# A routing step's scatter list moved ahead of filler products, and two one-element writes into the expert buffers' pool

## The chip, the core and the metric

The kernel runs on one core of one Trainium2 chip. The metric is the device time of one execution in microseconds (us); before and after are run several times on the same chip. The core's engines are TensorE (PE, with its weight loads shown apart as PEld), VectorE (DVE), ScalarE (ACT), GpSimd (POOL) and SyncE (SP), and 16 DMA engines move data between device memory and the core's memory. Each engine works through its own instructions in the order in which the program gives them.

## The reference

Linear attention with an exponential feature map feeds a mixture of eight experts. The part that this change touches is the second half:

```python
logits = x @ w_gate                      # x: 4608 tokens x 512
for idx in np.argsort(-logits.flatten()):
    tok, e = idx // E, idx % E
    if assigned[tok] >= 0 or counts[e] >= cap: continue   # cap = 4608 // 8 = 576
    assigned[tok] = e; counts[e] += 1
for e in range(E):
    mask = assigned == e
    h = np.maximum(x[mask] @ w1[e], 0.0)     # 512 -> 1024
    out[mask] = h @ w2[e]                    # 1024 -> 512
```

Every token goes to one expert and every expert takes exactly 576 tokens. The greedy rule is followed exactly, in eight rounds: a round finds the expert that fills up next, the threshold at which it does, and the list of its 576 tokens.

## The kernel before, in words

**Stages.** The attention part comes first and writes its result `xs` (4608 x 512) to device memory. Then `routing(0)` finds the first expert and its tokens. While expert `r` is computed, `routing(r+1)` runs between its instructions, mostly on VectorE. The first routing (`wide`) has nothing to run beside: nothing else can start until it has named an expert.

**What `routing(0)` does.** Six digits of the threshold are found one after the other (the loop over `i`): VectorE compares (L602), TensorE counts (L614), VectorE tests the counts (L631) and picks (L639, L643). Then the tokens are ranked and a list of 576 row numbers is made: compares against the low digit in `lo` (L701), 18 products with `hv` (L709) whose sum is copied to `pb` (L714), and eight small products (L719) that spread `pb` over the partitions. Two casts write the list into `idx[:,0:4]` and `idx[0:64,4]` (L720, L721). The list has five blocks: four of 128 tokens and a remainder of 64. The remainder's results are scattered as half rows, so the scatter needs a list of its own, `idx[:,5]`: four more products with one column (L742) and one VectorE instruction (L743). Only the scatter of the remainder reads it. Behind it stand the steps that take the expert's tokens out of the game (L744 to L752); they change `L`, from which `routing(1)` starts (L435).

**Fillers.** `idle(n)` (L581) issues n products on constant ones into a bank that nobody reads. Eleven of them stand between the eight list products (L719) and the four of the remainder (L742); four and three stand behind the first two transposes.

**The expert part.** `ga` (L852) gathers a block of rows from `xs` into `xg` with an indirect DMA that GpSimd issues; five gathers make an expert. Behind the second gather of expert 0 GpSimd copies the expert's number (L818), and on that copy SP waits before it issues the last two of the four parts of `w1` (`raww`, L766). ScalarE casts each part to its high half (`w1h`, L837) and VectorE forms the low half (`w1l`, L840, two instructions a part). For blocks 0 and 1 TensorE transposes `xg` (L882), ScalarE casts (`xh`, L895 and L894), VectorE subtracts (`xl`, L897); blocks 2 and 3 are transposed together (L887). The products of the first layer (L922) are three times split: `xh*w1h`, `xh*w1l`, `xl*w1h`. ScalarE applies the relu (`fh`, L935) and VectorE forms the low half (`fl`, L939), which also frees the PSUM bank. The second layer is L953, and the results are scattered by indirect DMAs (L983).

**Order.** The order of the expert part is written out by hand: a table gives every step a place, and each engine follows its own sequence. On ScalarE the casts of the third and fourth part of `w1` come ahead of the first relu. On VectorE the steps of `routing(1)` alternate with `w1l`, `xl` and `fl`. `up0`, which holds L742 to L752, is VectorE's first step.

**Pools.** The tiles of the expert part lie in the pool `fp`, which takes over memory of the attention part's tiles. The first instruction of an engine that writes a tile of `fp` therefore has to wait for the last users of that memory: other engines and many DMA queues. The small tiles of the routing lie in another pool (`rt`), which was there from the start. The tile `wk` is one of those: a GpSimd copy of one element (L705) that waits for the first group of `lo`.

Of the kernel before, what the change touches and what calls it, by code (L numbers as in the profile page):

```python
# [9 lines left out]
BF = mybir.dt.bfloat16  # L10
I32 = mybir.dt.int32
AF = mybir.ActivationFunctionType
OP = mybir.AluOpType
# [545 lines left out]
def moe(ctx, tc, nc, L, xs, w1, w2, out, C, MC, R0, rt, cfg={}):  # L559
# [3 lines left out]
    V,G,A,PE=nc.vector,nc.gpsimd,nc.scalar,nc.tensor  # L563
    rp=rt
    fp=ctx.enter_context(tc.tile_pool(name='ffn',bufs=2))
# [3 lines left out]
    def inner(x,n): return x.rearrange('p (t o) -> p t o',o=1).to_broadcast([x.shape[0],x.shape[1],n])  # L569
    def mid(x,t): return x[:,None,:].to_broadcast([x.shape[0],t,x.shape[1]])  # L570
# [3 lines left out]
    S=lambda shape,name,dt=F32,b=1: rp.tile(shape,dt,name=name,bufs=b)  # L574
    def rps(shape): return ps.tile(shape,F32,name='rps',bufs=cfg.get('rps',2))
# [6 lines left out]
    def routing(r):  # L582

        last = r==E-1
        wide = r<cfg.get('wide',1)
        if not last:
            R=R0 if r==0 else state()
            if r: yield from prep(R,0,NT)
            dg,OH=R['dg'],R['OH']
            c=dg[:,0]; lat=cfg.get('lat0',1.2)  # L590
            for i,(sh,bits) in enumerate(DIG):
                K=KW[i]; n=128//K; fin=i==ND-1
                part='n0' in R and i==0
                if part:
                    p=rps([8,K])
                    cnt0(R,p,NT//9-1,cmp0(R,NT//9-1),True,True)
                else:
                    cmp=S([128,NT//n,K,n],f'cmp{K}',BF,b=2)
                    cv=c.rearrange('p (g i) -> p g i',i=n)
                    g=0  # L600
                    for ck in ((WC if K==32 else WC2) if wide else (9,)*(1 if K==32 else 2)):
                        V.tensor_tensor(cmp[:,g:g+ck],cv[:,g:g+ck,None,:].to_broadcast([128,ck,K,n]),  # L602
                                        kt[i].rearrange('p (k i) -> p k i',i=n)[:,None].to_broadcast([128,ck,K,n]),op=OP.is_ge); g+=ck
                if 'rest' in R:
                    with tc.issue_after(R['last']):
                        if i: 
                            for _ in R.pop('rest'): pass
                        else: next(R['rest'])
                yield
                if part: pass  # L610
                elif wide:
                    p=rps([8,K])
                    for t in range(NT):
                        PE.matmul(p,OH[:,t,:],cmp[:,t//n,:,t%n],start=t==0,stop=t==NT-1)  # L614
                else:
                    p=rps([128,n,8])
                    for g in range(NT//n):
                        PE.matmul(p,cmp[:,g].rearrange('p k i -> p (k i)'),OH[:,g*n:g*n+n,:],start=g==0,stop=g==NT//n-1)  # L618
                    yield
                    mm=S([128,n,8],f'mm{n}'); V.tensor_mul(mm,p,msk[n])  # L620
                    V.tensor_reduce(tin[:,0:8].rearrange('p (e o) -> p e o',o=1),mm.rearrange('p i e -> p e i'),axis=AX.X,op=OP.add)
                    tr=S([128,32],'tr'); V.transpose(tr,tin)
                    yield
                    cn8=S([128,32//n,1],f'cn{n}'); V.tensor_reduce(cn8,tr.rearrange('p (k i) -> p k i',i=n),axis=AX.X,op=OP.add)
                    f32=S([128,32//n],f'f{n}'); V.tensor_scalar(f32,cn8[:,:,0],float(cap),2.0**(-7*i),op0=OP.is_ge,op1=OP.mult)
                    ds8=S([128,1],'ds'); V.tensor_reduce(ds8,f32,axis=AX.X,op=OP.add)
                if wide:
                    fl=S([8,K],f'fl{K}',BF); da=S([8,1],'da',BF)
                    with nc.allow_low_precision(reason='counts up to 64'):
                        if part: V.scalar_tensor_tensor(fl,p,-float(cap),R['n0'],op0=OP.add,op1=OP.is_ge,accum_out=da)  # L630
                        else: V.tensor_scalar(fl,p,float(cap),0.0,op0=OP.is_ge,op1=OP.add,accum_out=da)  # L631
                else:
                    fl=S([128,8],'fl128',BF); V.tensor_scalar(fl,eye8,ds8,None,op0=OP.mult)
                yield
                p=rps([128,8])
                if wide: PE.matmul(p,da.to_broadcast([8,128]),e8s[:,i],start=True,stop=True)
                else: PE.matmul(p,ones,fl,start=True,stop=True)
                if r: yield
                ch=S([128,1],'ch'); V.tensor_reduce(ch,p,axis=AX.X,op=OP.max)  # L639
                lat=cfg.get('latd',.7)  # L640
                if fin: break
                c2=S([128,NT],'cc',BF,b=2)
                V.scalar_tensor_tensor(c2,c,ch,dg[:,i+1],op0=OP.subtract,op1=OP.add); c=c2  # L643
                if r: yield

            f8=S([128,8],'f8')
            V.scalar_tensor_tensor(f8,p,ch,e8,op0=OP.is_equal,op1=OP.mult)
            c1=S([128,1],'c1'); V.tensor_scalar(c1,ch,-2.0**(-7*(ND-1)),None,op0=OP.add)
            mx=S([128,1],'mx'); V.tensor_reduce(mx,f8,axis=AX.X,op=OP.max)
        else:  # L650
            f8=S([128,8],'f8'); V.tensor_mul(f8,opn,e8)
            mx=S([128,1],'mx'); V.tensor_reduce(mx,f8,axis=AX.X,op=OP.max)
# [19 lines left out]
        p=rps([128,2,NT])  # L672
# [23 lines left out]
        if r: yield  # L696
        lo=S([128,18,64,2],'cmp64',BF,b=2)
        l2=sf[:,0].rearrange('p (g i) -> p g i',i=2)
        lk=6 if wide else 9
        for g in range(0,18,lk):  # L700
            V.tensor_tensor(lo[:,g:g+lk],l2[:,g:g+lk,None,:].to_broadcast([128,lk,64,2]),  # L701
                            kl.rearrange('p (k i) -> p k i',i=2)[:,None].to_broadcast([128,lk,64,2]),op=OP.is_equal)
        if wide:

            wk=S([1,1],'wk',BF); G.tensor_copy(wk,lo[0:1,0,0,0:1])  # L705
        yield
        p=rps([128,9,2,2])
        for g in range(18):
# [2 lines left out]
        idx=S([128,6,1],'idx',I32,b=3)  # L711
        if wide:

            pb=S([128,9,2,2],'pb',BF); V.tensor_copy(pb,p)  # L714
            p=rps([128,5])
            for j in range(4):
                for o in (0,64):
                    k=5 if o==0 else 4
                    PE.matmul(p[o:o+64,0:k],dup2[:,j%2,o:o+64],pb[:,o//64:9:2,j//2,j%2],start=j==0,stop=j==3,skip_group_check=True)  # L719
            V.tensor_copy(idx[:,0:4,0],p[:,0:4])  # L720
            V.tensor_copy(idx[0:64,4,0:1],p[0:64,4:5])  # L721
        else:

            pm=S([128,9,2,2],'pm')
            V.tensor_mul(pm,p,msk[2][:,:,0][:,None,None,:].to_broadcast([128,9,2,2]))
            d9=S([128,9,2,1],'d9',BF)
            with nc.allow_low_precision(reason='under 64, and multiples of 64 up to 71 times 64'): V.tensor_reduce(d9,pm,axis=AX.X,op=OP.add)
            yield
            p=rps([128,9,2])
            PE.matmul(p,dup.rearrange('p i a -> p (i a)'),d9[:,:,:,0],start=True,stop=True)  # L730
            yield
            pr=S([128,9,2],'pr'); V.tensor_copy(pr,p)
            V.tensor_add(idx[0:64,0:5,0],pr[0:64,0:9:2,0],pr[0:64,0:9:2,1])
            V.tensor_add(idx[64:128,0:4,0],pr[64:128,1:9:2,0],pr[64:128,1:9:2,1])
            r8=S([128,1],'r8'); V.tensor_add(r8,pr[:,8,0:1],pr[:,8,1:2])
            V.tensor_scalar(idx[:,5],r8,2.0,half,op0=OP.mult,op1=OP.add)
        T['idx',r]=idx
        if not last:
            yield 'up'
            if wide:  # L740
                p=rps([128,1])
                for j in range(4): PE.matmul(p,dup2[:,j%2],pb[:,8:9,j//2,j%2],start=j==0,stop=j==3)  # L742
                V.tensor_scalar(idx[:,5],p,2.0,half,op0=OP.mult,op1=OP.add)  # L743
            E1=S([128,8],'E1'); V.tensor_scalar(E1,f8,mx,None,op0=OP.is_equal)  # L744
            mem=S([128,NT],'mem'); g1=S([128,NT],'g1')
            V.tensor_add(g1,gt[:,0],gt[:,1])
            V.scalar_tensor_tensor(mem,si,12288+cap-.5,g1,op0=OP.is_lt,op1=OP.mult)
            V.tensor_sub(un,un,mem)
            V.tensor_sub(opn,opn,E1)
            pen=S([128,NT,8],'sc')  # L750
            V.tensor_tensor(pen,inner(mem,8),mid(E1,NT),op=OP.max)
            V.scalar_tensor_tensor(L,pen,-1.0e38,L,op0=OP.mult,op1=OP.add)  # L752
    BL=[(b*128,min(128,cap-b*128)) for b in range(5)]
    ctx.enter_context(tc.manual_schedule())

    it0=routing(0)
    for x in it0:
        if x=='ei':
# [296 lines left out]
```

## Time and profile before

| | |
|---|---|
| time, median of 3 runs | 763.65 us (763.33 to 764.94) |
| time of the profiled execution | 765.09 us |
| its span, first to last instruction | 763.2 us |
| TensorE products busy | 736.1 us (96%) |
| TensorE weight loads busy | 633.3 us (83%) |
| VectorE busy | 571.4 us (75%) |
| ScalarE busy | 348.2 us (46%) |
| GpSimd busy | 312.0 us (41%) |
| mean granted TensorE clock | 0.977 |

The profiled execution is read in microseconds from its first instruction. Attention ends near 277 us, the first routing near 301 us, and the first expert's products begin at 307 us. A busy share is an average over stages with different limits; what the change touches lies between 277 and 330 us.

### The profile page before, as it was taken

How to read it: one execution, taken by the hardware profiler on the slowest of the kernel's cores; microseconds unless marked ns; L12 is line 12 of the kernel's file. 1: busy time of each engine (PE TensorE's matmuls, PEld its weight loads, DVE VectorE, ACT ScalarE, POOL GpSimd, SP SyncE). 2: the span in 40 equal slices, each digit the busy share in tenths (PEclk: the TensorE clock that was granted, in tenths of full speed). 3: DMA queues.
4: the chain of work that ended last, by engine and by line, in shares of the span. 5: the costliest groups of instructions: out<-in, count | busy, mean ns of one | idle time of the engine just before them, and what ended most of it. 6: DMA issues, size and time to landing. Idle time of an engine off the chain costs nothing.

```text
span 763.2 us, 25319 instructions
## 1 busy us (share of the span) xinstructions
PE 736.1 (96%) x10832; PEld 633.3 (83%) x10832; DVE 571.4 (75%) x1495; ACT 348.2 (46%) x612; POOL 312.0 (41%) x336
## 2 busy tenths in 40 slices
PE   7999999999999966999999999999999999999997
PEld 3888888998898864788897897897897897897985
DVE  5999899989997975996796796796796795673410
ACT  2677677877788431333522422422422422542411
POOL 6797888988889701103103103103103103312002
PEclk9999999999999985999999999999999999999999
DMA  9979688988883032325405405406405406662301
GB/s 168 153 136 154 132 166 165 165 142 156 156 167 81 13 86 75 104 107 186 160 1 182 164 2 183 163 1 186 160 1 184 163 2 198 236 190 60 132 15 49
DMA packets 236944, 94.28 MB, mean 124 GB/s; under 512 B 185904, under 2 KB 223184, under 8 KB 236832
## 3 DMA queue, kind: packets, MB, share of 16 engines
q1 hardware_dynamic: 225552, 71.91, 40.4%
q0 software_dynamic: 6608, 20.16, 8.3%
q8 instruction: 85, 1.39, 0.8%
q10 hardware_dynamic: 4672, 0.59, 0.6%
q14 instruction: 27, 0.22, 0.1%
HBM read 72.58 MB, written 20.05 MB: 121 GB/s over the span
## 4 chain that ended last, share of the span: by engine, by line
PE 65%; issue 13%; DVE 12%; POOL 4%; ACT 2%; SPq 2%; DMA 1%; POOLq 0%; DVEq 0%
PE h L922 22%; PE y L953 18%; PE g L293 8%; DVE kgm L189 4%; PE y L968 3%; PE g L185 3%; PE g L276 2%; PE g L231 2%; SPq L122 2%; DVE qgt L192 2%; DVE qgm L189 2%; PE rps L618 2%; POOL ks L222 1%; PE g L247 1%; PE h L887 1%
## 5 line engine op out<-in xcount | busy, mean ns | idle before, releaser
L983 POOL DMA_INDIRECT out_dram<-ysb,idx x40 | 39.2, 981 | 335.9 <-ACT ysb L976 329.9
L222 POOL TENSOR_TENSOR ks<-ks,kP 128x512 f32<-128x512 f32 x112 | 143.2, 1279 | 7.4 <-ACT kP L213 0.2
L922 PE MATMUL h<-xh,w1l 128*128 128x272 f32 (+3 forms) x512 | 142.0, 297 | 0.3 <-DVE w1l L840 0.2
L922 PE MATMUL h<-xh,w1h 128*128 128x272 f32 (+3 forms) x512 | 141.6, 302 | 0.1
L935 ACT ACTIVATE fh<-h 128x272 fp32r<-128x272 f32 (+2 forms) x128 | 49.1, 384 | 136.6 <-PE h L922 128.8
L953 PE MATMUL y<-w2h,fh 128*128 128x512 f32 x256 | 101.2, 398 | 0.0
L953 PE MATMUL y<-w2l,fh 128*128 128x512 f32 x256 | 99.9, 395 | 0.0
L953 PE MATMUL y<-w2h,fl 128*128 128x512 f32 x256 | 99.3, 392 | 0.0
L922 PEld LDWEIGHTS h<-xh,w1l 128*128 128x128 f32 x512 | 97.1, 190 | 1.8 <-DVE w1l L840 0.8
L922 PEld LDWEIGHTS h<-xh,w1h 128*128 128x128 f32 x512 | 96.0, 190 | 2.0 <-issue 0.4
L922 PE MATMUL h<-xl,w1h 128*128 128x272 f32 (+3 forms) x512 | 93.3, 299 | 1.1 <-DVE xl L897 1.1
L213 ACT ACTIVATE kP<-kgt 128x768 f32<-128x768 f32 x96 | 73.9, 837 | 34.0 <-POOL kgt L201 19.0
L939 DVE SCALAR_TENSOR_TENSOR fl<-h,fh 128x272 fp32r<-128x272 f32 (+2 forms) x128 | 53.0, 416 | 38.7 <-ACT fh L935 22.2
L293 PE MATMUL g<-kz,qP 128*64 128x73 f32 x2304 | 78.9, 229 | 2.0 <-DVE kz L262 1.8
L293 PEld LDWEIGHTS g<-kz,qP 128*64 128x64 f32 x2304 | 76.3, 138 | 3.8 <-DVE kz L262 1.9
L280 ACT ACTIVATE qP<-g 128x768 f32<-128x768 f32 x96 | 70.9, 813 | 16.1 <-PE g L276 16.1
L922 PEld LDWEIGHTS h<-xl,w1h 128*128 128x128 f32 x512 | 76.5, 190 | 1.8 <-DVE xl L897 1.3
L231 PE MATMUL g<-kP,vi 64*64 64x256 f32 x1152 | 70.5, 377 | 0.1
L976 ACT COPY ysb<-y 128x512 f32<-128x512 f32 (+1 forms) x40 | 21.8, 546 | 100.5 <-issue 59.2
L953 PEld LDWEIGHTS y<-w2l,fh 128*128 128x128 f32 x256 | 48.2, 188 | 9.0
L953 PEld LDWEIGHTS y<-w2h,fl 128*128 128x128 f32 x256 | 48.2, 188 | 8.8
L953 PEld LDWEIGHTS y<-w2h,fh 128*128 128x128 f32 x256 | 48.3, 189 | 8.3
(220 smaller groups left out, 1314.7 us busy)
## 6 DMA issues: line engine op xcount, KB each, us to landing
raww<-in_moe_w_dram SPq DMA_DIRECT2D x64, 512.0 KB, 5.2
xs<-xp SPq DMA_DIRECT2D x32, 288.0 KB, 4.7
ki<-in_k_dram SPq DMA_DIRECT2D x62, 144.0 KB, 3.9
qi<-in_q_dram SPq DMA_DIRECT2D x62, 144.0 KB, 4.0
vi<-in_v_dram SPq DMA_DIRECT2D x56, 144.0 KB, 4.1
vi<-in_v_dram POOLq DMA_DIRECT2D x8, 144.0 KB, 7.2
xl<-xd SPq DMA_DIRECT2D x4, 288.0 KB, 4.3
xd<-xg SPq DMA_DIRECT2D x4, 256.0 KB, 3.5
```

What stands on the lines that cost most here:

```text
L185: PE.matmul(p[64*bi:64*bi+64,a,128*(s-s0):128*(s-s0)+128],t[r,bi,s,:],C['w'][r,:],start=True,stop=True)
L189: V.tensor_reduce(m,vw(),axis=AX.X,op=OP.max,apply_absolute_value=True)
L213: for i in range(2): A.activation(o[:,:,:,128*i:128*i+128],t,AF.Exp,scale=1.0-2*i)
L222: else: G.tensor_add(ks,ks,kP[:,s])
L231: PE.matmul(p[64*a:64*a+64,i,0:256],v_[r,a,s,:],kP[r,s,a,:],start=s==0,stop=s==8,skip_group_check=True)
L280: for fh in range(2): A.activation(t[:,fh].rearrange('p i a s t -> p i (a s t)'),p,AF.Exp,scale=1.0-2*fh)
L293: PE.matmul(p[64*ab:64*ab+64,a,73*(j-j0):73*(j-j0)+73],T['qP',u,j//3][:,fh,a,ab,j%3,:],T['kz',u][:,a,fh,ab,:],start=fh==0,stop=fh==1)
L922: PE.matmul(p,ws[:,k,o:o+128],xx[:,k,o1:o2],start=n==0,stop=n==11)
L935: A.activation(hh[:,f,o1:o1+m1],p[:,0:m1],AF.Relu)
L939: V.scalar_tensor_tensor(hl[:,f,o1:o1+m1],p[:,0:m1],0.0,hh[:,f,o1:o1+m1],op0=OP.max,op1=OP.subtract)
L953: PE.matmul(p,hx[:,f,o:o+128],ws[:,f%2,:],start=n==0,stop=n==23)
L983: st=G.indirect_dma_start(out=ov,out_offset=bass.IndirectOffsetOnAxis(ap=iv,axis=0),in_=yv,in_offset=None)
```

## The change

Four edits. The four products and the VectorE instruction that make `idx[:,5]` move from behind the eleven fillers to the place behind the eight list products, under the same `routing(0)`. The tile `wk` moves from the routing's pool to `fp`. In the fourth of the six digit steps (`i==3`) VectorE writes a zero into a new one-element tile `wv` of `fp`. The 18 rows of `lo` are compared in groups of 7, 7 and 4 instead of three of 6.

```diff
@@ routing, the loop over the digits @@
                         V.tensor_tensor(cmp[:,g:g+ck],cv[:,g:g+ck,None,:].to_broadcast([128,ck,K,n]),
                                         kt[i].rearrange('p (k i) -> p k i',i=n)[:,None].to_broadcast([128,ck,K,n]),op=OP.is_ge); g+=ck
+                if wide and i==3: V.memset(fp.tile([1,1],BF,name='wv',bufs=1),0.0)
@@ routing, the list @@
-        lk=6 if wide else 9
-        for g in range(0,18,lk):
+        g0=0
+        for lk in (7,7,4) if wide else (9,9):
+            g=g0; g0+=lk
             V.tensor_tensor(lo[:,g:g+lk],l2[:,g:g+lk,None,:].to_broadcast([128,lk,64,2]),
                             kl.rearrange('p (k i) -> p k i',i=2)[:,None].to_broadcast([128,lk,64,2]),op=OP.is_equal)
         if wide:
-            wk=S([1,1],'wk',BF); G.tensor_copy(wk,lo[0:1,0,0,0:1])
+            wk=fp.tile([1,1],BF,name='wk',bufs=1); G.tensor_copy(wk,lo[0:1,0,0,0:1])
@@ behind the eight list products @@
+            p5=rps([128,1])
+            for j in range(4): PE.matmul(p5,dup2[:,j%2],pb[:,8:9,j//2,j%2],start=j==0,stop=j==3)
             V.tensor_copy(idx[:,0:4,0],p[:,0:4])
             V.tensor_copy(idx[0:64,4,0:1],p[0:64,4:5])
+            V.tensor_scalar(idx[:,5],p5,2.0,half,op0=OP.mult,op1=OP.add)
@@ behind the fillers @@
             yield 'up'
-            if wide:
-                p=rps([128,1])
-                for j in range(4): PE.matmul(p,dup2[:,j%2],pb[:,8:9,j//2,j%2],start=j==0,stop=j==3)
-                V.tensor_scalar(idx[:,5],p,2.0,half,op0=OP.mult,op1=OP.add)
```

## Rows read from the trace of the kernel before

**Rows 1.** Windows: us, PE, PEld, DVE, ACT, POOL busy; clock, DMA share, GB/s
```profile
311.00:314.50 3.50, 3.50 (x18) 3.50 (x19) 3.50 (x13) 1.41 (x3) 0.00 (x0) 0.52 0.20 69
...
320.00:330.00 10.00, 9.90 (x89) 9.51 (x88) 9.20 (x33) 3.66 (x10) 0.00 (x0) 1.00 0.58 211
...
352.00:400.00 48.00, 48.00 (x420) 42.55 (x418) 37.25 (x126) 19.21 (x43) 8.59 (x13) 1.00 0.31 110
```

**Rows 2.** Timeline, TensorE: start us, us, line, tile, count, idle before and releaser
```profile
300.28 4.51 PE L581 MATMUL y<-onesb 128*128 128x512 bf16 x11
304.63 0.24 PE L742 MATMUL rps<-pb,dup 128*128 128x1 bf16 x4
304.98 0.66 PE L882 MATMUL h<-ident,xg 128*128 128x128 f32 x4
...
307.37 0.41 PE L922 MATMUL h<-xh,w1h 128*128 128x256 f32 x1
...
310.88 1.04 PE L922 MATMUL h<-xl,w1h 128*128 128x256 f32 x4 [1.06 <-DVE xl L897]
...
316.95 0.71 PE L887 MATMUL h<-ident,xg 64*128 64x64 f32 x16
...
318.77 0.28 PE L922 MATMUL h<-xh,w1l 128*128 128x256 f32 x1
```

**Rows 3.** Timeline, VectorE, the first routing and the first expert
```profile
286.55 0.18 DVE L631 TENSOR_SCALAR_CACHE_REDUCE fl<-rps 8x32 bf16<-8x32 f32 x1 [0.73 <-PE rps L614]
...
300.38 0.16 DVE L720 CAST idx<-rps 128x4 int32<-128x4 f32 x1 [0.47 <-PE rps L719]
...
304.91 0.22 DVE L743 TENSOR_SCALAR idx<-rps,half 128x1 int32<-128x1 f32 x1 [4.30 <-PE rps L742]
...
307.13 0.69 DVE L840 TENSOR_TENSOR w1l<-raww,w1h 128x512 fp32r<-128x512 f32 x1 [0.31 <-issue]
...
310.15 0.68 DVE L897 TENSOR_TENSOR xl<-h,xh 128x512 fp32r<-128x512 f32 x1
...
313.83 0.75 DVE L602 TENSOR_TENSOR cmp<-dg,kt 128x1152 bf16<-128x1152 bf16 x1
314.74 0.76 DVE L939 SCALAR_TENSOR_TENSOR fl<-h,fh 128x256 fp32r<-128x256 f32 x2 [0.16 <-ACT fh L935]
...
316.26 0.19 DVE L620 TENSOR_TENSOR mm<-rps,msk 128x32 f32<-128x32 f32 x1 [0.17 <-PE rps L618]
...
317.92 0.69 DVE L840 TENSOR_TENSOR w1l<-raww,w1h 128x512 fp32r<-128x512 f32 x1
```

**Rows 4.** Timeline, GpSimd: gathers of experts 0 and 2, a scatter
```profile
301.47 1.06 POOL L852 DMA_INDIRECT xg<-xs,idx  x1 [2.63 <-DMA raww<-in_moe_w_dram]
...
305.44 0.95 POOL L852 DMA_INDIRECT xg<-xs,idx  x1 [0.30 <-issue]
...
346.85 1.02 POOL L983 DMA_INDIRECT out_dram<-ysb,idx  x1 [39.14 <-ACT ysb L976]
...
414.73 1.50 POOL L852 DMA_INDIRECT xg<-xs,idx  x1 [0.30 <-issue]
```

**Rows 5.** Timeline, ScalarE, the same stretch, and the copy ahead of that scatter
```profile
300.91 1.99 ACT L837 CAST w1h<-raww 128x1024 fp32r<-128x1024 f32 x2 [2.81 <-DMA raww<-in_moe_w_dram]
305.67 0.59 ACT L895 CAST xh<-h 128x512 fp32r<-128x512 f32 x1 [2.78 <-PE h L882]
307.05 0.77 ACT L894 CAST xh<-h 128x128 fp32r<-128x128 f32 x4 [0.79 <-PE h L882]
...
313.37 1.04 ACT L837 CAST w1h<-raww 128x1024 fp32r<-128x1024 f32 x1 [2.09 <-DMA raww<-in_moe_w_dram]
...
345.98 0.59 ACT L976 COPY ysb<-y 128x512 f32<-128x512 f32 x1 [3.85 <-PE y L953]
```

**Rows 6.** Timeline, SP's queue: the last two parts of w1 are issued
```profile
304.80 0.94 SPq L766 DMA_DIRECT2D raww<-in_moe_w_dram  x2
```

**Rows 7.** Chain of work that ended last: start us, us, what
```profile
299.32 0.37 PE rps L709 x6
```

## The prediction

> **What bounds the kernel now.** I read the busy shares first (TensorE 96%), then the windows by stage, then the chain of waits, then the timelines of the five engines from 286 to 320 us. TensorE's share is an average. In expert 1's stage it is busy 48.00 of 48.00 us, and from 320 to 330 us 9.90 of 10.00, with VectorE at 9.20 beside it [rows 1]. So a microsecond won before 320 us stays won to the end. Around the change other things set the pace, and the reader should see four.
>
> First, VectorE stands still for 4.30 us because the four products of the remainder's list wait behind eleven fillers: idx is written at 300.38 + 0.16 = 300.54, the next VectorE instruction starts at 304.91 [rows 2, 3]. Second, TensorE pays for that later: it reaches the xl products and waits 1.06 us for VectorE, whose second xl ends at 310.15 + 0.68 = 310.83 [rows 2, 3]. Behind this wait it runs at a granted clock of 0.52, which is the lower of its two levels for nearly all of 311 to 314.5 us: 18 products in 3.50 us (0.19 each), against 89 in 9.90 (0.11) at 320 to 330 [rows 1]. Third, the first fl at 314.74 waits for ScalarE [rows 3], and ScalarE had stood before the fourth part of w1, which arrived at 313.37 [rows 5]; the relus are queued behind its cast. Fourth, that part had been issued by SP from 304.80 on [rows 6], and SP's issue hangs on the GpSimd copy behind the second gather.
>
> **The change, part by part.**
>
> *Remainder's list moved.* The four products cost 0.24 us [rows 2]. They now push the fillers back by that and no longer stand behind them: the sum on TensorE before the first transposes is the same, they stay at 304.9 instead of 304.98 [rows 2]. If the products cost double at the low clock, the fillers end 0.24 later and so do the transposes: bounds 0.1 us won to 0.25 lost there. On VectorE L743 can start when its products end, near 300.65 (behind the second idx cast), 4.25 us sooner than 304.91. The steps behind it, to the first w1l, take 307.13 - 0.31 - 304.91 = 1.91 us [rows 3]; VectorE is at w1l at 302.6. The high half is there: ScalarE's two casts run from 300.91 for 1.99 us, so the first ends near 301.9 [rows 5].
>
> *Where those 4.25 us go.* xl needs xh. The first xh ends at 305.67 + 0.59 = 306.26, the four small casts of the second at 307.05 + 0.77 = 307.82 [rows 5]; both follow the transposes, which hardly move (0.07). So the second xl starts at 307.8 and ends at 308.5 instead of 310.83: 2.3 us are left. TensorE starts its first products at 307.3 (307.37 less 0.07), has eleven to do before xl, 11 x 0.11 = 1.2, and arrives at 308.5: the wait of 1.06 is gone. Then comes the next late one. VectorE goes from the end of xl to the end of the compare in 313.83 + 0.75 - 310.83 = 3.75 us [rows 3], at 312.25, and finds no fh: fl started 314.74 - 313.37 = 1.37 us after the fourth part landed [rows 3, 5], in ScalarE's order it can't be sooner, and the transposes of blocks 2 and 3 (316.95 before [rows 2]) wait for fl to free their banks. TensorE is there near 312.8 and waits. From here on only an earlier landing counts.
>
> *wk in the expert pool.* The first gather starts 301.47 - 300.54 = 0.93 us behind its list [rows 3, 4]. The timeline names a DMA as what it waited for, which had nothing to do with the list; I read it as a row of waits for the pool's former users that stands ahead of the gather. wk takes these waits in the 2.63 - 0.93 = 1.7 us before the list is ready, when GpSimd has nothing else to do; nothing but the gathers is queued behind it. With the list as its last wait a gather should start like the scatter that waits for its copy alone: 346.85 - (345.98 + 0.59) = 0.28 us [rows 4, 5]. That is 0.65 us won; the other bound is nothing, if only instructions long since passed are moved. I take 0.6 with the next edit, nearer the scatter, since wk leaves only the list and the last stores of xs to wait for. All five gathers, the copy and SP's issue move by it.
>
> [...] VectorE's work of 305 to 308 us now falls on the first gathers. The rows: the first gather takes 1.06 us with VectorE idle, the fourth 0.95 with VectorE busy, but one of expert 2's takes 1.50 [rows 4]. By the last, a stretched second gather gives back 0.54 us, and the copy behind it moves by 0.06 instead of 0.6; by the first two nothing is lost. I take the first two, because they are the same expert's. Below as a rival.
>
> *wv.* A zero and the waits ahead of it, at most the 0.31 us that the first w1l shows, fall into 0.73 us in which VectorE waits for the counts of that digit [rows 3]. Cost 0; without the cover 0.4 on the path. What it gives, 0.25 us before w1l, is swallowed by the wait for xh. If a former user were still at work at 286 us it would be late, but attention has been over for 9 us.
>
> *Groups of 7, 7 and 4.* The same elements on VectorE. The last group of products, 6 in 0.37 us [rows 7], becomes 4; a sixth of it each, at most 0.12 us, more likely 0.06 since they overlap; at worst 0.1 lost because the first group is later. It moves the list and so the gathers.
>
> **Sum.** The fourth part lands 0.6 us sooner, at 312.75; fl starts at 314.1. Behind it VectorE's 0.17 us of waiting for counts at 316.26 [rows 3] is gone too, since TensorE has done them. The w1l that ended at 317.92 + 0.69 ends 0.77 sooner, and the product that needs it, at 318.77 [rows 2] only 0.16 behind it, runs 0.8 us sooner. Behind that VectorE has almost no idle time, so TensorE cannot get further ahead. 765.09 - 0.8 = 764.3 for the profiled execution, which is 1.44 above the median of 763.65; on the median's footing **762.85 us**. What a measurement of this kernel tells from no change is about 0.2%, 1.5 us, so this is "no change" by that measure.
>
> The new wait, some 1.5 us ahead of the transposes of blocks 2 and 3, may bring the low clock as the 1.06 us did. Between those transposes and the product at 318.77 lie 1.82 us of work [rows 2], up to 3.5 at the low clock: it would end by 318.1, against the 318.0 of the sum. This costs 0.1 to 0.3 us.
>
> **Rivals.**
>
> *The weights are not in the way.* The fourth part landed 313.37 - 304.80, over 7 us, after its issue [rows 5, 6], while the first two arrived by 301.9; its slow end could vanish when the gathers are out of the way. Then VectorE keeps its lead of 2.3 us to fl: gain 1.6 to 2.4, 761.5 as its middle. Against it: gathers and weights move together, so they meet as before.
>
> *The gathers don't start sooner* (the waits cost nothing where they were, or VectorE stretches the second gather by 0.54). The landing stays within 0.1 of 313.37, VectorE's lead is lost there, and 0.2 remains: 763.45. For it: GpSimd had 1.7 us for these waits already. In its first form wk does not do what it says.
>
> *Slower: a low clock where TensorE sets the pace.* If the wait ahead of the transposes of blocks 2 and 3 brings the clock down late, past 318 us, a stretch of 3.5 us like that of 311 to 314.5 loses 3.5 x (1 - 0.11/0.19) = 1.5 us behind the place where anything hides it. It decides from a fall after 317.5 on. With the 0.8 won this is +0.7, 764.35; with only 0.2 won, +1.3, 764.95. Against it: the low stretch before began right behind its wait.
>
> **How the numbers follow.** Forecast 0.50, own range 762.3 to 763.5. Weights not in the way 0.16, gathers not sooner 0.22, slower 0.12. The range of eight in ten goes from 761.4 (the middle of the second case) to 764.3 (the usual slower case). Faster by over 0.2%: the second case and a part of the forecast's edge, 0.18. Slower by over 0.2%: half of the slower case, 0.06. Within: 0.76.
>
> **What would show it.** In the profile after: L743 near 300.7 without idle time; the first gather near 300.8 and 0.3 behind the idx cast; SP's issue near 304.2; no wait of TensorE for xl near 308.5 and full clock through 311; VectorE idle some 1.8 us ahead of fl; the fourth part's cast near 312.8; TensorE waiting over a microsecond ahead of L887. The prediction is wrong if that cast starts before 312 or not before 313.3, or if the low clock lies behind 318 us.

## The result, and the profile after

The change makes the kernel slower: 772.0 us median (770.15 to 773.10, 6 runs) against 764.2 for the kernel before on the same chip; ratio 1.0094, 95% interval 1.0076 to 1.0112. The forecast was 762.85 us, its range ended at 764.3, and slower had a chance of 0.06. The profiled execution took 773.05 us with a span of 771.0, that is 7.8 us more span than before.

First the windows by stage, since they say where the 7.8 us lie. Columns: the window, its length, then busy us and count of PE, PEld, DVE, ACT and POOL, granted clock, DMA share, GB/s. The DMA share adds up the times of the packets and divides by 16 engines; packets overlap, and so it stands above 1 in places (1.26 and 1.29 just below). After:

```profile
0.00:20.00 20.00, 15.26 (x159) 8.64 (x163) 11.38 (x22) 4.33 (x5) 13.58 (x23) 0.93 1.26 136
20.00:40.00 20.00, 14.81 (x340) 12.02 (x334) 14.40 (x20) 9.34 (x13) 10.54 (x9) 0.90 1.29 141
```

The same two windows of the kernel before, which no row ahead of the prediction shows:

```profile
0.00:20.00 20.00, 15.27 (x155) 8.44 (x159) 11.12 (x22) 4.33 (x5) 13.32 (x23) 0.94 1.09 169
...
20.00:40.00 20.00, 19.18 (x497) 16.20 (x495) 19.93 (x28) 14.34 (x20) 15.16 (x13) 0.98 0.94 153
```

From 20 to 40 us TensorE is busy 14.81 us in place of 19.18, while the DMA engines are busier (1.29 for 0.94) and move less (141 GB/s for 153). Not one instruction of this stage was changed. The DMA view of the first 280 us says which transfers. After (queue: packets, MB, share of 16 engines; then issues, KB each, median us from issue to landing):

```profile
q1 hardware_dynamic: 195744, 35.40, 79.4%
...
ki<-in_k_dram SPq DMA_DIRECT2D x62, 144.0 KB, 4.8
qi<-in_q_dram SPq DMA_DIRECT2D x62, 144.0 KB, 4.7
```

Before:

```profile
DMA packets 201551, 38.45 MB, mean 137 GB/s; under 512 B 183424, under 2 KB 201213, under 8 KB 201485
...
q1 hardware_dynamic: 196093, 35.58, 71.0%
...
ki<-in_k_dram SPq DMA_DIRECT2D x62, 144.0 KB, 3.9
qi<-in_q_dram SPq DMA_DIRECT2D x62, 144.0 KB, 4.0
```

Almost the same packets and bytes take 79.4% of the engines' time, not 71.0%, and a load of k lands after 4.8 us, not 3.9. The packets' times in these two traces, by size, say which: those of 128 bytes (k and q) took 15.5 ns on average, before 13.3, and so 49.5% of the engines' time in place of 42.4, which is 7.2 of the 8.4 points. Those of 256 bytes (v) add 1.7, those of 512 (`xs`) add nothing. VectorE's transposes of k then wait 7.7 us for their data instead of 2.8. The stage ends late, as the last stores of `xs` show (SP's timeline by line; first and last start in the window), after and then before:

```profile
L315 SPq DMA_DIRECT2D xs<-xp x3: 574/639/1206, 274.6 to 285.6; - x3
```

```profile
L315 SPq DMA_DIRECT2D xs<-xp x2: 574/606/639, 277.8 to 278.4; - x2
```

285.6 - 278.4 = 7.2 us of the 7.8 are lost before the first routing begins. From that store to the end it takes 771.0 - 285.6 = 485.4 us, before 763.2 - 278.4 = 484.8. So the part that the change touches, which I had forecast 0.8 faster, is 0.6 longer in these two executions. That is less than the 1.0 us by which executions with the old routing differ among themselves (483.8 to 484.8 in the kernel before and runs 2 to 5 below), so it is not shown to be slower.

In that part the steps can be read on the old axis by taking 7.2 off. GpSimd's timeline after:

```profile
305.96 0.28 POOL L707 COPY wk<-cmp 1x1 bf16<-1x1 bf16 x1 [30.43 <-DVE cmp L703]
308.04 1.07 POOL L853 DMA_INDIRECT xg<-xs,idx  x1 [1.81 <-DVE idx L725]
```

VectorE's timeline after:

```profile
307.60 0.16 DVE L724 CAST idx<-rps 128x4 int32<-128x4 f32 x1 [0.47 <-PE rps L721]
...
307.80 0.22 DVE L726 TENSOR_SCALAR idx<-rps,half 128x1 int32<-128x1 f32 x1
...
320.76 0.76 DVE L940 SCALAR_TENSOR_TENSOR fl<-h,fh 128x256 fp32r<-128x256 f32 x2 [1.73 <-ACT fh L936]
```

ScalarE's timeline after:

```profile
319.40 1.05 ACT L838 CAST w1h<-raww 128x1024 fp32r<-128x1024 f32 x1 [1.39 <-DMA raww<-in_moe_w_dram]
```

TensorE's timeline after:

```profile
315.54 0.64 PE L923 MATMUL h<-xl,w1h 128*128 128x256 f32 x4
...
321.24 1.04 PE L888 MATMUL h<-ident,xg 64*128 64x64 f32 x16 [0.97 <-DVE fl L940]
...
323.83 0.17 PE L638 MATMUL rps<-fl,onesb 128*128 128x8 bf16 x1 [1.00 <-DVE fl L634]
...
324.53 0.41 PE L923 MATMUL h<-xh,w1h 128*128 128x256 f32 x1
324.74 0.41 PE L923 MATMUL h<-xh,w1l 128*128 128x256 f32 x1
```

The gather starts 308.04 - 307.76 = 0.28 us behind its list, before it was 0.93 [rows 3, 4]. The remainder's list stands at 307.80 without idle time, 300.6 on the old axis, where it was 304.91 [rows 3]. TensorE's wait of 1.06 us for xl [rows 2] is gone. The fourth part of w1 is cast at 319.40, 312.2 on the old axis, 1.2 sooner than the 313.37 of [rows 5]: SP issues that part 0.5 sooner (312.07, 304.9 on the old axis, before 305.36) and it lands 7.3 us after its issue instead of 8.0. Then come two waits, 0.97 us for fl and 1.00 for the digit's count, and behind them the products of TensorE run 324.74 - 324.53 = 0.21 us apart instead of 0.12 (starts at 319.53 and 319.65, ahead of the waits). The windows show it as the lower of the two clock levels in these two traces (0.50 from 325 to 330 us, 1.00 from 316 to 322):

```profile
324.00:331.50 7.50, 7.50 (x44) 6.86 (x45) 5.44 (x19) 1.14 (x3) 0.00 (x0) 0.54 0.11 26
```

By the timeline it lasts from 324.3 to 331.0: 6.7 x (1 - 0.12/0.21) = 2.9 us lost, by this estimate.

### The profile page after: what moved, and what is told of

Its sections match the earlier page's. It is cut to its first block, busy times and chain, and to the rows that moved or that the text cites. A ratio compares the mean times of both kernels' runs of the same rounds, so it can differ in the third digit from the quotient of the medians.

```text
span 771.0 us, 25322 instructions
## 1 busy us (share of the span) xinstructions
PE 738.6 (96%) x10832; PEld 638.0 (83%) x10832; DVE 572.3 (74%) x1496; ACT 348.2 (45%) x612; POOL 312.0 (40%) x336
## 4 chain that ended last, share of the span: by engine, by line
PE 70%; issue 12%; DVE 8%; SPq 3%; DMA 2%; POOL 2%; ACT 1%; POOLq 0%; DVEq 0%
PE h L923 21%; PE y L954 18%; PE g L293 9%; PE g L185 5%; PE g L231 4%; PE y L969 3%; DVE kgm L189 3%; SPq L122 3%; PE g L276 2%; PE rps L619 1%; PE g L247 1%; DVE qgm L189 1%; DVE qgt L192 1%; PE rps L615 1%; PE g L260 1%
```

## The experiments

**What the change did to the attention.** In the built programs `wk` took 32 bytes in the routing's pool. The tiles that lie behind it in that pool and all tiles of the attention lie 32 bytes lower after the change: `ki` at 61664 instead of 61696, `qi` at 70880 instead of 70912. 61696 is 241 x 256 and 70912 is 277 x 256. k and q are loaded in pieces of 32 floats, 128 bytes, so before the change no piece lay across a multiple of 256 in SBUF, and after it every second one does. The first four runs ask whether it is the addresses, which tiles', and which step counts (64 or 256 bytes). A line below is a name for a stretch of 256 bytes that starts at a multiple of 256; whether such a boundary costs anything is what the runs ask. An unused pad tile moves addresses and adds no instruction.

**1. The changed kernel with the 32 bytes put back.**

```diff
-            wk=fp.tile([1,1],BF,name='wk',bufs=1); ...
+            S([1,1],'pad',BF); wk=fp.tile([1,1],BF,name='wk',bufs=1); ...
```

> The changed kernel with one edit: an unused 32-byte tile stands in the routing's pool where wk stood, so that the attention tiles behind it have their former addresses. Theory A (the addresses of the attention tiles cost the time): attention ends at 277.8 us as before instead of 285.0, and the execution takes 764 to 765.5 us, since the rest of the trace of the changed kernel is 0.5 us longer than before. Rival B (the edits in the routing and the expert part cost the time, or the instructions that were added): 772 us as in the changed kernel.

764.11 us median, ratio 0.9981 (0.9963 to 0.9999). The attention is back, with the last store of `xs` at 279.2:

```profile
20.00:40.00 20.00, 18.51 (x484) 15.37 (x476) 19.47 (x28) 14.07 (x20) 14.61 (x13) 0.99 0.93 152
```

```profile
q1 hardware_dynamic: 195792, 35.43, 71.0%
```

So nearly all of the change's loss is an address. What is left of the change is worth 0.0019 x 765.2 = 1.5 us (0.1 to 2.8; 765.2 is the median of the kernel before beside it). ScalarE's and then TensorE's timeline show that the fourth part of w1 is 2.8 us earlier counted from the last store (311.34 - 279.2 = 32.1, before 313.37 - 278.4 = 35.0), and that TensorE has one short wait:

```profile
311.34 1.05 ACT L838 CAST w1h<-raww 128x1024 fp32r<-128x1024 f32 x1 [0.49 <-DMA raww<-in_moe_w_dram]
```

```profile
316.65 0.17 PE L638 MATMUL rps<-fl,onesb 128*128 128x8 bf16 x1 [0.54 <-DVE fl L634]
```

The clock is 1.00 from 314 to 322 us.

**2 and 3. The kernel before, its attention tiles 32 or 64 bytes higher.**

```diff
-            wk=S([1,1],'wk',BF); ...
+            S([1,16],'pad',BF); wk=S([1,1],'wk',BF); ...
```

(32 elements in the second.)

> The kernel before with an unused 32-byte tile in the routing's pool, so that all attention tiles lie 32 bytes higher; no instruction changes. Theory A: attention about 7 us longer, 771 to 772 us. Rival B: 764.2 us as before.

> The kernel before with an unused 64-byte tile in the routing's pool. Theory A1 (a piece of a load must start at a multiple of 64 bytes): 764.2 us as before. Theory A2 (the 128-byte pieces of the loads must not cross a multiple of 256 bytes; half of them do now, as in the changed kernel): 771 to 772 us. Rival B: 764.2 us.

32 bytes: 1.0094 (1.0072 to 1.0116), q1 77.9%. 64 bytes: 1.0069 (1.0046 to 1.0092), q1 79.3%. A shift alone, with nothing of the change, costs what the change cost. That 64 bytes cost too speaks against steps of 64 bytes and for longer lines.

**4. Only `ki` and `qi` off the lines**, by a pad of 32 bytes in front of them and one behind; the other attention tiles move by 64.

```diff
+    sb.tile([128,16],BF,name='pada',bufs=1)
     for nm,x in (('k',k),('q',q)): loadx(nm,x,0,(nc.sync,nc.scalar))
+    sb.tile([128,16],BF,name='padb',bufs=1)
```

> The kernel before with two unused 32-byte tiles, one ahead of the tiles ki and qi and one behind them: only the places into which q and k are loaded lie at odd multiples of 32 bytes, the other attention tiles are shifted by 64. Theory A with the loads of q and k as its place: 771 to 772 us, the loads land later (near 4.8 us instead of 3.9) and TensorE is busy below 16 of the 20 us from 20 to 40. If instead the engines are slower on tiles at such addresses (kT, kP, ks and so on): 764.2 us.

1.0099 (1.0069 to 1.0130). Windows and DMA view:

```profile
20.00:40.00 20.00, 14.64 (x328) 11.87 (x324) 14.13 (x20) 8.75 (x13) 10.87 (x9) 0.89 1.30 138
```

```profile
q1 hardware_dynamic: 195744, 35.40, 80.3%
```

The tiles of the routing and of the experts lie where they lay, so the cost comes from the attention's tiles. By itself the run does not single out those of k and q, since the others lie 64 bytes higher, as in run 3, which cost as well. The packets do: those of 128 bytes took 15.7 ns on average and 50.0% of the engines' time (13.3 ns and 42.4% in the kernel before), again most of the rise from 71.0 to 80.3%.

**5. The kernel before, 128 bytes higher**: the tiles begin at 128 beyond the start of a line. Their pieces fill the two halves of a line in turn, as before, and none lies across two.

```diff
+            S([1,64],'pad',BF); wk=S([1,1],'wk',BF); ...
```

> The kernel before with 128 bytes put in front of the list's last small tile, so that every attention tile lies 128 bytes higher. The 128-byte pieces of q and k then begin at 128 beyond a multiple of 256 and again none crosses a 256-byte line. Theory (crossings of 256-byte lines cost the attention its loads): ratio 0.998 to 1.002, PE busy from 20 to 40 us near 19, mean DMA share near 0.94, landing of k near 3.9 us. Rival (any shift from the old addresses disturbs the hand-made schedule): ratio 1.007 to 1.010 as with 32 and 64 bytes, PE near 15, share near 1.25, landing near 4.8 us.

0.9994 (0.9982 to 1.0007), no change:

```profile
20.00:40.00 20.00, 18.71 (x466) 15.04 (x459) 18.57 (x27) 13.97 (x19) 13.77 (x12) 0.95 0.96 149
```

```profile
q1 hardware_dynamic: 195744, 35.40, 71.7%
```

Shifts of 32 and 64 cost 0.7 to 0.9%, one of 128 nothing: what costs is that 128-byte pieces lie across a boundary, not that addresses moved. Runs 1 to 5 would come out alike if the boundaries stood every 128 bytes, since then every piece of the shifted kernels would lie across one. The packets of v speak for 256: in run 2 `vi` lies at 128 beyond a multiple of 256, and 21% of its packets took over 18 ns, while on the lines (run 11) 1% did. This is not shown for sure, since k and q were slow in run 2 as well. (The landing of k, 4.5 us, came out nearer the rival's number; share, windows and time did not.)

**6. The list alone.** The kernel before with the four products, `idx[:,5]` and nothing else of the change.

```diff
+            p5=rps([128,1])
+            for j in range(4): PE.matmul(p5,...)
...
+            V.tensor_scalar(idx[:,5],p5,2.0,half,op0=OP.mult,op1=OP.add)
...
-            if wide:
-                p=rps([128,1])
...
```

> The kernel before with the remainder's four products and its scatter list moved ahead of the fillers, and nothing else of the change; addresses as before. Theory (as in the prediction): TensorE's wait of 1.06 us for xl goes, the lead stops at the first fl, because the fourth part of w1 lands as before, 8 us behind its issue; gain about 0.2 us, ratio 0.999 to 1.000. Rival (the list is what won the 1.5 to 2.5 us of the padded kernel): ratio 0.997 to 0.998, the fl products as early as in the padded kernel.

1.0024 (1.0008 to 1.0039): slower, which neither theory had. The mechanism is the predicted one, the price is not. TensorE's timeline:

```profile
309.02 0.64 PE L921 MATMUL h<-xl,w1h 128*128 128x256 f32 x4
...
314.25 1.04 PE L886 MATMUL h<-ident,xg 64*128 64x64 f32 x16 [0.49 <-DVE fl L938]
...
316.84 0.17 PE L637 MATMUL rps<-fl,onesb 128*128 128x8 bf16 x1 [1.00 <-DVE fl L633]
```

and the windows:

```profile
317.20:320.40 3.20, 3.20 (x20) 2.77 (x19) 2.80 (x7) 0.37 (x1) 0.00 (x0) 0.50 0.00 0
```

No wait for xl, the lead stops at fl, and behind the waits lies a stretch at the lower clock, here 3.2 us of it. Over its 12 runs the mean granted clock averages 0.974, over the 35 of the kernel before beside them 0.978. The profiled execution, 764.86, is one of its faster ones (764.12 to 769.73); of its runs the fastest, 764.12, had a mean granted clock of 0.979, the slowest, 769.73, one of 0.967.

**7. All but the list.** Run 1 with the list put back behind the fillers: `wk` in `fp`, `wv`, and 7, 7, 4.

```diff
-            p5=rps([128,1])
-            for j in range(4): PE.matmul(p5,...)
...
+            if wide:
+                p=rps([128,1])
...
```

> The padded kernel with the remainder's list put back behind the fillers: left are wk in the expert pool, wv, and the groups of 7, 7 and 4, with the attention's addresses as before. Theory (the copy in the expert pool brings gathers and weights forward): first gather 0.28 us behind the idx cast, fourth part of w1 cast over 1 us earlier than before, but VectorE reaches xl as late as before and TensorE waits 1 us for it; gain 0.2 to 0.8 us, ratio 0.999 to 1.000. Rival (the waits alone are worth the padded kernel's gain): ratio 0.997 to 0.998.

0.9996 (0.9984 to 1.0007). The first gather starts 299.61 - (299.16 + 0.16) = 0.29 us behind its list, as with the whole change, but TensorE waits as before:

```profile
309.04 0.74 PE L924 MATMUL h<-xl,w1h 128*128 128x256 f32 x4 [1.07 <-DVE xl L899]
```

So neither half shows a gain alone; together, on the old addresses, they gain 1.5 us (run 1), though that interval overlaps this run's.

**8. The list, and two relus ahead of the cast.** If the list's lead is lost because the relus of fl are queued behind the cast of w1's fourth part, their order on ScalarE is the cure.

```diff
-'w1h.0.3': 13.01, 're.0.0.0': 13.96, 're.0.1.0': 14.24,
+'re.0.0.0': 13.96, 're.0.1.0': 14.24, 'w1h.0.3': 14.3,
```

> The kernel with the list alone moved, and in ScalarE's order the first two relus of expert 0 put ahead of the cast of w1's fourth part. Theory (the lead won by the list is lost at fl, because the relus are queued behind that cast; TensorE's two waits behind it, 0.49 and 1.00 us in the run with the list alone, bring the low clock of 317 to 320 us): fl starts over 0.7 us sooner without waiting for ScalarE, TensorE's waits ahead of the transposes and of the digit's count shrink, the granted clock stays near 1.00 from 314 to 322 us, ratio to the kernel before 0.997 to 1.000. Rival (something else makes the list cost time): waits and low clock as with the list alone, ratio 1.001 to 1.004.

0.9978 (0.9965 to 0.9991), 762.6 us median against 766.5 for the list alone. ScalarE's timeline:

```profile
311.86 0.64 ACT L934 ACTIVATE fh<-h 128x256 fp32r<-128x256 f32 x2
313.00 1.05 ACT L836 CAST w1h<-raww 128x1024 fp32r<-128x1024 f32 x1 [0.50 <-DMA raww<-in_moe_w_dram]
```

The windows behind it:

```profile
314.00:318.00 4.00, 3.13 (x36) 2.70 (x32) 3.83 (x13) 2.02 (x6) 0.00 (x0) 1.00 0.00 0
318.00:322.00 4.00, 3.90 (x38) 3.70 (x37) 3.79 (x16) 0.82 (x3) 0.00 (x0) 1.00 0.12 28
```

fl starts at 312.5 without waiting, TensorE's wait for fl is gone, that for the count is 0.59 us, and the clock stays at 1.00. So the relus' place behind the cast is what stopped the lead. That the low clock was the price of the list alone is argued, not shown by itself: the clock averages 0.978 over these 10 runs, 0.979 in the kernel before beside them, and 0.974 in run 6.

**9. Only the relus' order**, in the kernel before; same edit.

> The kernel before with the two relus ahead of the cast of the fourth part and nothing else. Theory (in the kernel before VectorE came to fl only 0.16 us before ScalarE's relu; the order pays only behind the moved list): ratio 0.9985 to 1.0005, TensorE's wait of 1.06 us for xl and the low clock of 311 to 314.5 us stay. Rival (the order alone gave the gain of the kernel with list and order): ratio 0.996 to 0.9985.

1.0003 (0.9990 to 1.0015). The order gives nothing without the list, as expected. One part of the expectation failed: TensorE's wait for xl is there (1.06 us), but no low clock follows it in this execution (1.00 from 311 to 314 us).

**10. Only the relus' order, in the changed kernel.**

> The changed kernel with the same two relus ahead of the cast of the fourth part. Theory (its low clock behind 324 us comes from the same wait): fl without a wait, the clock near 1.00 from 322 to 332 us, 1.5 to 3 us sooner from the last store of the attention to the end; the attention as long as in the changed kernel; ratio to the kernel before 1.005 to 1.008. Rival (the low clock has another cause): ratio 1.008 to 1.011.

1.0054 (1.0037 to 1.0070), so 0.004 x 764 = 3.1 us of the change's loss are mended without touching addresses. The clock is at 1.00 where the changed kernel had 0.50:

```profile
326.00:330.00 4.00, 4.00 (x31) 3.90 (x32) 3.79 (x15) 0.51 (x3) 0.00 (x0) 1.00 0.14 49
```

The last store of `xs` starts at 285.8, as late as in the changed kernel; from there to the end it takes 767.9 - 285.8 = 482.1 us instead of 485.4.

**11. v on the lines too.** Run 1 with 160 bytes in front of `vi`. v comes in pieces of 256 bytes (64 floats) and `vi` lay at 96 beyond a line, so each piece lay across one.

```diff
+        if u==0: sb.tile([128,80],BF,name='padv',bufs=1)
         t=T['v',u]=sb.tile([128,2,9,D],F32,name='vi',bufs=2)
```

> The padded kernel with 160 more bytes in front of the tile of v, so that its pieces of 256 bytes begin at a multiple of 256; before each of them lay across a 256-byte line. Theory (crossings cost DMA time): landing of v falls from 4.1 us toward 3.5, the queue's share in the first 280 us falls below 71%; where DMA share is 0.93 TensorE gains: last store of the attention 0.5 to 3 us earlier, ratio to the kernel before 0.993 to 0.998. Rival (the loads of v are not in the way, or a whole piece across one line costs nothing): landing of v 4.1 us, ratio 0.997 to 0.999 as the padded kernel.

0.9970 (0.9957 to 0.9982). q1's share of the first 280 us falls as expected:

```profile
q1 hardware_dynamic: 196141, 35.61, 68.4%
```

The trace lacks the landings. The attention is hardly shorter (last store 278.2), and the time is not separated from run 1's 0.9981: the DMA time is shown, a gain from it is not. The trace shows one thing more. TensorE has the changed kernel's two waits, almost as long, and its clock does not fall:

```profile
313.69 1.04 PE L889 MATMUL h<-ident,xg 64*128 64x64 f32 x16 [0.88 <-DVE fl L941]
...
316.27 0.17 PE L639 MATMUL rps<-fl,onesb 128*128 128x8 bf16 x1 [0.99 <-DVE fl L635]
```

```profile
313.00:322.00 9.00, 6.89 (x67) 6.11 (x68) 8.37 (x31) 3.23 (x9) 0.00 (x0) 1.00 0.07 3
```

From the last store to the end it takes 761.2 - 278.2 = 483.0 us, in the changed kernel 485.4.

**12. Run 11 with the relus' order of run 8**, to see whether the gains add.

> The padded kernel with v on the 256-byte lines and the two relus ahead of the cast of the fourth part. Theory: both gains add, ratio 0.993 to 0.997. Rival (in the padded kernel the fourth part lands so early that the order changes nothing): ratio 0.996 to 0.998 as with v on the lines alone.

760.15 us median, 0.9946 (0.9925 to 0.9967), the best of all and faster than both kernels. The interval overlaps run 11's, so that the gains add is not shown. Its profile still has a wait of 1.25 us for the count and a low clock:

```profile
314.00:322.00 8.00, 7.35 (x53) 6.87 (x53) 6.96 (x23) 1.50 (x5) 0.00 (x0) 0.79 0.16 51
```

So the order does not cure the clock in every case.

## Why the prediction was wrong, step by step

**The step that failed is "wk in the expert pool".** It priced the move as waits alone ("nothing but the gathers is queued behind it") and never asked what a tile's leaving does to those behind it in the pool it leaves. A shift of 32 bytes costs 0.9% by itself (run 2, upwards); with the 32 bytes put back the change costs nothing (run 1). The term that the prediction put at nothing was worth 7.2 us. None of its signs looks at the attention: read as they stand, they all miss by about 7 us (the fourth part's cast at 319.40, not 312.8), and the cause shows only ahead of 280 us. The runs show the cost where no instruction changed and only places in SBUF moved (run 2: 0.9%, q1's share 77.9% for 71.0); the 128-byte packets took 15.7 ns on average in run 4 and 15.5 in the changed kernel, before 13.3. Why a piece that lies across two lines takes longer is not shown. For pieces that start off a line without lying across two the runs show next to no cost: in the kernel before every second piece of k and q starts at 128 beyond a line, and 95% of the 128-byte packets took 13 ns or less.

**"Remainder's list moved" and "Where those 4.25 us go" were right as a chain**: list at once, no wait for xl, VectorE idle ahead of fl (1.73 us, forecast 1.8), TensorE standing ahead of the transposes (0.97, forecast some 1.5 and at least over 1). Run 8 shows the named reason, relus behind the cast. One premise did not hold: the low clock behind the wait for xl [rows 1] belongs to that one execution. Six other traces have the wait, 1.06 or 1.07 us, at full clock (1.00; runs 2 to 5, 7 and 9).

**The low clock was mis-sized.** The prediction gave 0.1 to 0.3 us for it, and its rival, which I gave 0.12, a stretch of 3.5 us and +0.7 in sum. I had not seen the second wait, 1.00 us for the count, which follows fl on VectorE. In the changed kernel the low stretch begins at 324.3, 317.1 on the old axis, just short of the rival's 317.5, but most of it lies behind 318, which the prediction had named as a sign of being wrong; it lasts 6.7 us and costs 2.9 by the estimate above. Run 10 gets 3.3 us of span back. The list alone is slower by 0.24% (run 6). In run 11, with the same edits and nearly the same two waits, the clock stayed up, so this price is not paid in every execution.

**The gathers' 0.65 us were right**: 0.28 or 0.29 us behind the list, in the changed kernel and in runs 1 and 7. What they are worth in time is not shown: run 7 can't be told from no change. The gathers were not stretched to 1.50 us, as one rival had it: in the changed kernel the second took 1.09 us and the third 1.24, before 0.96 and 0.97; that VectorE's work lengthens a gather, no run shows. `wv` is hidden as forecast: it lies at 293.21 and the next wait for counts is 0.55 us instead of 0.73. The groups of 7, 7 and 4 were not tried alone.

**The sum for the touched part**, -0.8 us, lies within what run 1 shows on the old addresses (-1.5, interval -2.8 to -0.1). From the last store to the end the traces with the whole change take 482.3 us (run 1), 483.0 (run 11) and 485.4 (the changed kernel, with the low clock), those with the old routing 483.8 to 484.8. Run 1's profile resembles more the rival "weights not in the way": the fourth part lands 5.7 us after its issue, not 8.0, and VectorE keeps its lead. In the changed kernel the same transfer took 7.3, and in the other traces that have it 6.7 to 8.2, so 5.7 is the shortest of ten executions. Run 11 looks like the forecast again, with VectorE idle 1.65 us ahead of fl. Why run 1 differs stays open; besides the attention, the expert tiles too lie 32 bytes apart in run 1 and the changed kernel, and the fillers met the gathers at different clocks. It wasn't tried.

## What to carry to other kernels

A tile that is added, removed or moved to another pool can move everything allocated behind it: list the addresses before and after, and look at the loads with small pieces, though no instruction of theirs has changed. Before a stall is removed, follow the lead it frees to the next late thing, here a relu queued behind a cast: two edits of which one costs 0.24% alone (run 6) and the other gains nothing (run 9) gain 0.2% together (run 8). A stall that moves to where TensorE has no slack can cost more by its clock than by its length (in the changed kernel 2.9 us, as estimated above, against two waits of 1.97 in sum), and one profile does not tell whether it will (run 11: no loss by the clock).

## What the runs showed of the hardware that was not expected

Whether 128-byte pieces lie across 256-byte lines of SBUF is worth between 6 and 10 points of the DMA queue's share: 70.8 to 71.8% in the seven traces with k and q on the lines and `vi` off them (the kernel before, runs 1 and 5 to 9), 77.9 to 80.3% in the five with every second piece across (the changed kernel, runs 2 to 4 and 10). A load of k lands after 3.9 to 4.5 us in the first, 4.7 to 5.0 in the second. That the lines are 256 bytes long rests on the packets of v (run 5) and is not shown for sure. Not every such piece is slow: in the changed kernel half of them lie across a line, and 22% of the packets took over 13 ns, before 5%.

In these traces TensorE's clock does not follow a stall of given length. Behind a wait of 1.06 to 1.07 us for xl it fell in the kernel before (0.52 from 311 to 314.5 us, [rows 1]) and stayed at 1.00 in runs 2 to 5, 7 and 9. Behind the wait for the count it stayed up after 0.53 to 0.63 us (runs 1, 3 to 5 and 7 to 10), 0.95 (run 2) and 0.99 (run 11), and fell after 1.00 (the changed kernel, run 6) and 1.25 (run 12). Since run 11 and the changed kernel differ by less than 0.1 us in each of their waits, these rows give no length that decides.
